# One maximum operation over two PSUM banks per step, three banks for exponentials and dense products, FFN weights in twelve transfers, lag of six steps: an attention and GEGLU block on one core

## The chip, the cores and the metric

The kernel runs on one core of a Trainium2 chip, in one launch. The metric is the device time in microseconds (us), the median of the runs shown. All times come from the kernel's timed runs or from one execution that the hardware profiler took.

## The reference

One transformer block over 2048 tokens of width 512, in bf16, batch 1:

```python
def reference(A_x, A_wqkv, A_wo, B_x, B_w_gate, B_w_up, B_w_down):
    x = A_x
    h = x + A(layernorm(x), A_wqkv, A_wo)
    return h + B(layernorm(h), B_w_gate, B_w_up, B_w_down)

def A(x, wqkv, wo):           # 32 heads of 16
    q, k, v = heads(x @ wqkv)
    p = softmax(q @ k.T * 16 ** -0.5)      # over all 2048 keys
    return (p @ v) @ wo

def B(x, w_gate, w_up, w_down):            # hidden width 1792
    return (gelu(x @ w_gate) * (x @ w_up)) @ w_down
```

## The kernel before

**Units and steps.** The attention is cut into 64 units: 8 groups of 256 queries (`gi`) times 8 slots of four heads (`slot`). A unit has 16 steps ("ticks"). The main loop (L1007 to L1042) runs over ticks and puts out, in each tick, work of two passes:

- **Pass 1**, `p1_pair` and `p1_consume`: two score products of 128 queries by 512 keys, for two heads, and the maximum of each over its 512 keys (L582, VectorE). After a unit's 16th tick, `negm_pre` takes the maximum over the four key blocks (L588), and four small GpSimd operations (L592 to L595) split its negative into three bf16 parts in `ST`. `negm_post` transposes `ST` into `STG` by a DMA (L601) and copies three rows per head from `STG` into spare rows of `QT` by four DMAs (L604). So the scores of pass 2 come out with the maximum already subtracted.
- **Pass 2**, `p2_pair` and `p2_consume`: the transposed scores of the unit again, in two tiles per tick, each of two products of 128 keys by 256 queries (L618); ScalarE takes the exponential of each tile of 128x512 (L628) into `PT`. Every fourth tick `pv_burst` multiplies eight such tiles with V (L644).

Pass 2 of a unit starts `16 + LAGX` ticks after its pass 1, here 26.

**The order on TensorE is written out.** A tick's products of both passes stand between `group_begin` and `group_end`. `group_end` (L108) gathers all semaphore waits of the group and puts them on its first instruction, so none of a tick's score products starts before every bank that the tick writes is free. Only the last product of each pass signals, so ScalarE starts when all four products of pass 2 are through. After the group comes one piece of "dense" work, or a burst of PV products, or, where there is neither, two dummy products (L1001).

**The dense work** is all else on TensorE: the projections of Q, K and V, the transposing back of attention outputs (`item_ofin`), the output projection (`item_oproj`), and for each finished group the FFN (`item_gate`, `item_up`, `item_down`). `Dense.piece()` advances one item by one piece per tick. From four ticks before pass 2 on, `dense.single` is set: an item takes one bank from `banks` when it starts and gives it back when its last piece is put out, and after an item two ticks pass (`PAUSE`). The item's result is taken from the bank by an extra ScalarE operation (`evac_act`), which is put out behind that tick's two exponentials. `item_down` of the first of two tiles takes its bank and then waits for seven ticks.

**The eight PSUM banks.** Banks 0 to 2 are a ring for pass 1, one bank per product (`p1_ring`). Banks 3, 4, 5 and 7 are `Banks.free`, a list out of which pass 2 takes two from the front in each tick, giving them back at its end when the exponentials have been put out, and from which a dense item takes its one. Bank 6 collects the PV products.

```python
while True:                                   # one tick
    P.group_begin("pe")
    t1 = p1_pair(...); t2l = p2_pair(...)     # p2_pair: banks.take() twice
    P.group_end("pe")
    p1_consume(...)                           # L582, and at a unit's end negm_pre, negm_post
    p2_consume(...)                           # L628, banks.give(b) after each
    cost = 0 if pv_tick else dense.piece()    # may take or give a bank
```

**Transfers.** All DMAs are issued by SyncE (SP), in program order; an issue waits for its inputs, and what stands behind it waits too. When the last projection has been put out, `qkv_finished` issues the three FFN weights as three transfers (L482 to L484), since they lie where the projections' operands were.

Of the kernel before, what the change touches and what calls it, by code (L numbers as in the profile page):

```python
# [196 lines left out]
GC = 0.7978845608028654  # L197

NPT = 12
LAGX = 10  # L200
PAUSE = 2


def bass_sequential_preLN__mha_block__geglu_ffn__prompt_kernel(nc, A_x, A_wqkv, A_wo, B_x, B_w_gate, B_w_up, B_w_down, out):
    dbg = None
    with ExitStack() as es:
# [156 lines left out]

        class Banks:
            def __init__(self):
                self.free = [3, 4, 5, 7]
            def take(self):
                return self.free.pop(0)
            def give(self, b):
# [109 lines left out]
        def qkv_finished():  # L479
            fk = [("xnT", t) for t in range(NT)] + ["wqkv"] + [(nm_, dc) for nm_ in ("wq_r", "wk_r") for dc in range(4)] + [("QKS", i_) for i_ in range(4)] + [("QKS2", i_) for i_ in range(2)]  # L480
            dF = rdeps("F", fk)
            P.dma("sp", lambda e: e.dma_start(out=wg_sb[:], in_=B_w_gate.rearrange("(c p) j -> p c j", p=128)), "wg", writes=["wg"], extra_deps=dF)  # L482
            P.dma("sp", lambda e: e.dma_start(out=wu_sb[:], in_=B_w_up.rearrange("(c p) j -> p c j", p=128)), "wu", writes=["wu"], extra_deps=dF)
            P.dma("sp", lambda e: e.dma_start(out=wd_sb[:], in_=B_w_down.rearrange("(c p) j -> p c j", p=128)), "wd", writes=["wd"], extra_deps=dF)  # L484

        qk_n = [0]
        qk_late = []
        def item_projT(b, which, ht, c):
            wr, nm = (wq_r, "wq_r") if which == "q" else (wk_r, "wk_r")
            for dc in range(4):  # L490
                P.op("pe", lambda e, dc=dc: e.matmul(pbank[:, b, :], wr[:, dc, 128 * ht:128 * ht + 128], xnT[:, dc, 512 * c:512 * c + 512], start=(dc == 0), stop=(dc == 3)),  # L491
                     reads=[(nm, dc)] + [("xnT", t) for t in range(4 * c, 4 * c + 4)], writes=[("pb", b)], sig=(dc == 3))
                if dc == 1:
                    yield 2
            si, s2 = qk_n[0] % 4, qk_n[0] % 2; qk_n[0] += 1
            def dst(slot):
                if which == "q":
                    return QT[:, c, slot, :], [("qT", slot, c)] + [("qTaug", slot, c, f_, g_) for f_ in range(2) for g_ in range(4)]
# [24 lines left out]
            qkv_left[0] -= 1  # L523
            if qkv_left[0] == 0:
                qkv_finished()
            return 2
# [38 lines left out]
        def p1_pair(ui, j, gp):  # L565
            gi, slot = units[ui]
            c, hf = gi // 2, gi % 2
            qt, kc = 2 * hf + j // 8, (j // 2) % 4
            tiles = []
            for jj in range(2):  # L570
                g = 2 * gp + jj
                b = p1_ring[0] % 3; p1_ring[0] += 1
                P.op("pe", lambda e, g=g, b=b: e.matmul(pbank[:, b, :], QT[32 * g:32 * g + 32, c, slot, 128 * qt:128 * qt + 128],  # L573
                                                        KT[32 * g:32 * g + 32, slot, 512 * kc:512 * kc + 512], start=True, stop=True, tile_position=(32 * g, 0)),
                     reads=[("qT", slot, c), ("qTaug", slot, c, hf, g), ("kT", slot, kc)], writes=[("pb", b)], sig=(jj == 1))
                tiles.append((b, j // 8, kc, g))
            return tiles

        def p1_consume(ui, tiles):
            par = ui % 2  # L580
            for (b, qt, kc, g) in tiles:
                P.op("dve", lambda e, b=b, qt=qt, kc=kc, g=g: e.tensor_reduce(out=PM[:, par, qt, kc, g:g + 1], in_=pbank[:, b, :], axis=AX.X, op=ALU.max),  # L582
                     reads=[("pb", b)], writes=[("PM", par, qt, kc, g)])

        def negm_pre(ui):
            par = ui % 2
# [10 lines left out]
        def negm_post(ui):  # L597
            gi, slot = units[ui]
            c, hf = gi // 2, gi % 2
            par = ui % 2  # L600
            P.dma("sp", lambda e: e.dma_start_transpose(out=STG[:, par, :].rearrange("p (q s) -> p q s", q=2), in_=ST[:, par].rearrange("p q s -> p (q s)")),  # L601
                  ("stT", par), reads=[("ST", par)], writes=[("STG", par)])
            for g in range(4):
                P.dma("sp", lambda e, g=g: e.dma_start(out=QT[32 * g + 16:32 * g + 19, c, slot, 256 * hf:256 * hf + 256], in_=STG[32 * g + 16:32 * g + 19, par, :]),  # L604
                      ("aug", par), reads=[("STG", par)], writes=[("qTaug", slot, c, hf, g)])

        pv_pending = []
        pt_n = [0]
# [1 line left out]
        def p2_pair(ui, j, gp):  # L610
            gi, slot = units[ui]
            c, hf = gi // 2, gi % 2
            m = j // 2
            tiles = [(banks.take(), m, 2 * gp + jj) for jj in range(2)]
            for i in range(2):
                kt = 2 * m + i
                for (b, _, g) in tiles:
                    P.op("pe", lambda e, g=g, b=b, kt=kt, i=i: e.matmul(pbank[:, b, 256 * i:256 * i + 256], KT[32 * g:32 * g + 32, slot, 128 * kt:128 * kt + 128],  # L618
                                                                        QT[32 * g:32 * g + 32, c, slot, 256 * hf:256 * hf + 256], start=True, stop=True, tile_position=(32 * g, 0)),
                         reads=[("qT", slot, c), ("kT", slot, kt // 4)] + [("qTaug", slot, c, hf, g_) for g_ in range(4)], writes=[("pb", b)],  # L620
                         sig=(i == 1 and g == 2 * gp + 1))
            return tiles

# [69 lines left out]
        def add_ffn(gi):  # L693
# [3 lines left out]
            for k in range(2):  # L697
                dense.add(item_down, gi, k, est=7)

        def load_xres(gi):  # L700
            assert gi < 2 or ffn_done.get(gi - 2), "dense stream too far behind (residual reuse)"
            for k in range(2):
# [15 lines left out]
        def post_hnT(gi, k):  # L718
# [2 lines left out]
                  ("hnT", 2 * gp + k), reads=[("OH", 2 * gp + k)], writes=[("hnT", gp, k)])  # L721
            hn_left[gi] = hn_left.get(gi, 2) - 1
            if hn_left[gi] == 0:
                defer(3, lambda: add_ffn(gi))

        def item_oproj(b, gi, k):
            gp, t = gi % 2, 2 * gi + k
# [71 lines left out]
        def gate_up_mms(b, gi, f, w, nm):  # L799
            hT = hnT_l[gi % 2]  # L800
            hr = [("hnT", gi % 2, k) for k in range(2)]
            for i in range(2):
                fc = 2 * f + i
                for dc in range(4):
                    P.op("pe", lambda e, dc=dc, fc=fc, i=i: e.matmul(pbank[:, b, 256 * i:256 * i + 256], w[:, dc, 128 * fc:128 * fc + 128], hT[:, dc, :], start=(dc == 0), stop=(dc == 3)),  # L805
                         reads=[nm] + hr, writes=[("pb", b)], sig=(dc == 3 and i == 1))
                if i == 0:
                    yield 2

# [37 lines left out]
        def down_mm(b, gi, k, fc):  # L847
            gp = gi % 2
            P.op("pe", lambda e: e.matmul(pbank[:, b, :], GUT[:, fc, 256 * gp + 128 * k:256 * gp + 128 * k + 128], wd_sb[:, fc, :], start=(fc == 0), stop=False),  # L849
                 reads=[("GUT", fc, gp), "wd"], writes=[("pb", b)], sig=False)  # L850
# [156 lines left out]
        while True:  # L1007
# [31 lines left out]
            if pv_tick:  # L1039
                pv_burst(8)  # L1040
            run_deferred(tick)
            tick += 1  # L1042
        run_deferred(tick, flush=True)
        tail_mode[0] = True
# [34 lines left out]
```

## Time and profile before

| | before |
|---|---|
| median of 2 runs | 1392.69 us (1392.41 to 1392.97) |
| profiled execution | 1393.8 us, span 1392.1 us |
| mean granted TensorE clock | 0.991 |
| busy: VectorE / ScalarE / TensorE / GpSimd | 1288.5 / 1235.2 / 1080.1 / 585.9 us |
| first and last product group of pass 1 | 34.4 and 1324.0 us |
| first and last product group of pass 2 | 71.0 and 1353.2 us |
| maxima over pass 1 tiles (L582) | 2048, 1248.9 us |
| exponentials (L628) | 2048, 1103.8 us |

The span is the time from the first to the last instruction of the profiled execution. Busy time is the time in which an engine works on at least one instruction; two instructions of an engine can overlap at their ends, so the mean duration of an instruction times the count is more than the busy time. A row of the timeline gives start, length, engine, line, operation, output and inputs, and in brackets how long the engine sat idle before it and what released it.

### The profile page before, as it was taken

The numbers are of one execution on the slowest core, as the hardware profiler recorded it, in microseconds if no ns is written. First come the engines' busy times: TensorE is split into PE (matmuls) and PEld (weight loads), VectorE is DVE, ScalarE is ACT, GpSimd is POOL, SyncE is SP. The second block draws the span as 40 slices with busy tenths as digits, with TensorE's granted clock in tenths as the row PEclk, the third lists the DMA queues.
The fourth block names the chain that finished last, engine by engine and source line by source line (L and its number), as shares of the span: only waits on it lengthen the run. The fifth ranks groups of instructions, "written<-read, shape, count | busy, mean of one in ns | idle before, by whom it ended". The sixth has DMA issues, their size and how long they took to land.

```text
span 1392.1 us, 33568 instructions
## 1 busy us (share of the span) xinstructions
PE 1080.1 (78%) x12464; PEld 372.1 (27%) x12682; DVE 1288.5 (93%) x2190; ACT 1235.2 (89%) x2409; POOL 585.9 (42%) x830
## 2 busy tenths in 40 slices
PE   4977757777787778777787778777787778877787
PEld 2222212223222222222222322222222322222224
DVE  5999969999999999999999999999999999999912
ACT  4499959999999999999999999899999999999991
POOL 4446611256313562236422662146512563145611
PEclk9999989999999999999999999999999999999999
DMA  3110040100010000000001000100001000100000
GB/s 121 42 29 24 26 164 6 29 5 4 10 21 17 4 6 13 21 11 6 6 13 26 6 6 9 23 13 6 4 13 29 6 3 10 25 14 3 6 15 12
DMA packets 50096, 28.00 MB, mean 20 GB/s; under 512 B 35600, under 2 KB 48400, under 8 KB 49936
## 3 DMA queue, kind: packets, MB, share of 16 engines
q1 hardware_dynamic: 49936, 25.84, 7.0%
q8 instruction: 103, 1.69, 0.5%
q14 instruction: 57, 0.47, 0.1%
HBM read 11.80 MB, written 2.10 MB: 10 GB/s over the span
## 4 chain that ended last, share of the span: by engine, by line
DVE 72%; PE 10%; ACT 8%; issue 7%; DMA 1%; POOL 1%; SPq 1%; POOLq 0%; ACTq 0%; DVEq 0%
DVE PM L582 70%; ACT PT L628 6%; PE pbank L573 3%; PE pbank L618 2%; PE pbank L644 1%; PE pbank L805 1%; DVE NEGM L588 1%; PE pbank L491 1%; PE pbank L849 1%; DVE stats L324 1%; ACT OA L467 1%; DMA OnT<-Otok 1%; PE pbank L730 1%; SPq L604 0%; DMA STG<-ST 0%
## 5 line engine op out<-in xcount | busy, mean ns | idle before, releaser
L582 DVE TENSOR_REDUCE PM<-pbank 128x1 f32<-128x512 f32 x2048 | 1248.9, 685 | 38.1 <-PE pbank L618 26.1
L628 ACT ACTIVATE PT<-pbank 128x512 bf16<-128x512 f32 x2048 | 1103.8, 613 | 87.1 <-PE pbank L618 24.6
L573 PE MATMUL pbank<-KT,QT 32*128 32x512 bf16 x2048 | 399.8, 383 | 208.8 <-DVE PM L582 148.4
L618 PE MATMUL pbank<-QT,KT 32*128 32x256 bf16 x4096 | 401.0, 273 | 2.3 <-ACT PT L628 2.2
L573 PEld LDWEIGHTS pbank<-KT,QT 32*128 32x128 bf16 x2048 | 109.2, 91 | 592.6 <-DVE PM L582 575.0
L1001 PE MATMUL pbank<-ones_bf,ident 128*128 128x512 bf16 x651 | 213.9, 384 | 36.8 <-ACT PT L628 28.9
L644 PE MATMUL pbank<-PT,VA 128*17 128x256 bf16 x4096 | 203.7, 276 | 18.8
L592 POOL CAST ST<-NEGM 128x8 bf16<-128x8 f32 x64 | 13.9, 218 | 318.6 <-DVE NEGM L588 318.6
L670 POOL TENSOR_TENSOR LINV<-OAT,negone 128x16 f32<-128x16 f32 (+1 forms) x32 | 92.0, 2876 | 92.9 <-ACT OAT L467 67.2
L618 PEld LDWEIGHTS pbank<-QT,KT 32*128 32x128 bf16 x4096 | 114.8, 92 | 11.2 <-ACT PT L628 7.0
L644 PEld LDWEIGHTS pbank<-PT,VA 128*17 128x17 bf16 x4096 | 56.5, 87 | 147.0 <-PE pbank L644 92.4
L781 POOL TENSOR_TENSOR w_sb<-g_sb 128x512 f32<-128x512 f32 x49 | 50.9, 1039 | 105.8 <-ACT g_sb L467 105.8
L1001 PEld LDWEIGHTS pbank<-ones_bf,ident 128*128 128x128 bf16 x826 | 49.8, 97 | 100.5 <-ACT PT L628 68.1
L805 PE MATMUL pbank<-hnT_l,wg_sb 128*128 128x256 bf16 x448 | 67.9, 277 | 1.8 <-issue 0.7
L805 PE MATMUL pbank<-hnT_l,wu_sb 128*128 128x256 bf16 x448 | 67.9, 277 | 0.0
L783 POOL TENSOR_TENSOR w_sb<-w_sb,g_sb 128x512 f32<-128x512 f32 x49 | 62.1, 1268 | 4.1
L787 POOL TENSOR_TENSOR th_sb<-th_sb,g_sb 128x512 f32<-128x512 f32 x49 | 62.0, 1264 | 4.1
L843 POOL TENSOR_TENSOR GUT<-th_sb,u_sb 128x512 bf16<-128x512 f32 x49 | 62.0, 1266 | 0.5
L849 PE MATMUL pbank<-wd_sb,GUT 128*128 128x512 bf16 x202 | 56.1, 381 | 5.5 <-PE pbank L618 2.0
L503 POOL TENSOR_SCALAR QT<-QKS,qmask 128x512 bf16<-128x512 bf16 x31 | 48.2, 1562 | 27.3 <-DMA QKS<-QKS 19.5
L786 POOL TENSOR_SCALAR th_sb<-th_sb 128x512 f32<-128x512 f32 x49 | 30.2, 617 | 68.3 <-ACT th_sb L795 68.3
L805 PEld LDWEIGHTS pbank<-hnT_l,wg_sb 128*128 128x128 bf16 x448 | 36.2, 98 | 27.7 <-issue 14.0
(112 smaller groups left out, 639.2 us busy)
## 6 DMA issues: line engine op xcount, KB each, us to landing
QT<-STG SPq DMA_DIRECT2D x256, 1.5 KB
QKS<-QKS SPq DMA_DIRECT2D x32, 112.0 KB, 2.2
x_sb<-in_A_x_dram SPq DMA_DIRECT2D x4, 512.0 KB, 5.6
xres<-in_A_x_dram SPq DMA_DIRECT2D x16, 128.0 KB, 2.2
out_dram<-out_sb SPq DMA_DIRECT2D x16, 128.0 KB, 1.8
wg_sb<-in_B_w_gate_dram SPq DMA_DIRECT2D x1, 1792.0 KB, 7.2
wu_sb<-in_B_w_up_dram SPq DMA_DIRECT2D x1, 1792.0 KB, 12.1
wd_sb<-in_B_w_down_dram SPq DMA_DIRECT2D x1, 1792.0 KB, 16.6
```

What stands on the lines that cost most here:

```text
L573: P.op("pe", lambda e, g=g, b=b: e.matmul(pbank[:, b, :], QT[32 * g:32 * g + 32, c, slot, 128 * qt:128 * qt + 128], KT[32 * g:32 * g + 32, ...
L582: P.op("dve", lambda e, b=b, qt=qt, kc=kc, g=g: e.tensor_reduce(out=PM[:, par, qt, kc, g:g + 1], in_=pbank[:, b, :], axis=AX.X, op=ALU.max ...
L618: P.op("pe", lambda e, g=g, b=b, kt=kt, i=i: e.matmul(pbank[:, b, 256 * i:256 * i + 256], KT[32 * g:32 * g + 32, slot, 128 * kt:128 * kt + ...
L628: P.op("act", lambda e, b=b, pi=pi: e.activation(out=PT[:, pi, :], in_=pbank[:, b, :], func=ACT.Exp), reads=[("pb", b)], writes=[("PT", pi)])
L644: P.op("pe", lambda e, g=g, kt=kt, pi=pi, slot=slot, i=i, col=col: e.matmul(pbank[32 * g:32 * g + 17, PVB, 256 * col:256 * col + 256], VA[ ...
L670: P.op("pool", lambda e: e.tensor_tensor(out=li, in0=oat4[:, :, :, 16], in1=negone[:, 0:8 * ns].rearrange("p (q h) -> p q h", q=2), op=ALU ...
L783: P.op(eng, lambda e: e.tensor_tensor(out=ws, in0=ws, in1=gs, op=ALU.mult), reads=[("w", par), ("g", par)], writes=[("w", par)])
L787: P.op(eng, lambda e: e.tensor_tensor(out=ts_, in0=ts_, in1=gs, op=ALU.mult), reads=[("th", par), ("g", par)], writes=[("th", par)])
L805: P.op("pe", lambda e, dc=dc, fc=fc, i=i: e.matmul(pbank[:, b, 256 * i:256 * i + 256], w[:, dc, 128 * fc:128 * fc + 128], hT[:, dc, :], st ...
L843: P.op("pool", lambda e: e.tensor_tensor(out=o_ap, in0=shp(ts_), in1=shp(us), op=ALU.mult), reads=[("th", par), ("u", par)], writes=o_keys ...
L849: P.op("pe", lambda e: e.matmul(pbank[:, b, :], GUT[:, fc, 256 * gp + 128 * k:256 * gp + 128 * k + 128], wd_sb[:, fc, :], start=(fc == 0), ...
L1001: P.op("pe", lambda e: e.matmul(pbank[:, b, :], ident[:], ones_bf[:, 0:512], start=True, stop=True), reads=["ident", "ones_bf"], writes=[( ...
```

## The change

Five things change together.

- **Pass 1** takes its banks in pairs: 0 and 1, then 2 and 3. One `tensor_reduce` takes the maxima of both banks of a tick (two outputs from 128x2x512) in place of two.
- **Bank 3** goes to pass 1, so the list that pass 2 and the dense items share has three banks, 4, 5 and 7.
- **The subtraction rows**: the four copies from `STG` into `QT` become one GpSimd addition of `STG` (128x256, bf16) onto the unit's half of `QT`.
- **LAGX** is 6 in place of 10.
- **The FFN weights** come in twelve transfers, four each, one at a time in ticks 7, 9, 11 and 13 of every 16; the FFN of a group is put on the list only when all twelve are issued.

```diff
-LAGX = 10
+LAGX = 6
...
-                self.free = [3, 4, 5, 7]
+                self.free = [4, 5, 7]
...
+            wviews = [(wg_sb, ..., "wg", 1), (wu_sb, ..., "wu", 1), (wd_sb, ..., "wd", 4)]
+            for (w, v, nm, step) in wviews:
+                n = w.shape[1]
+                for k in range(0, n, step):
+                    w_pieces.append((w, v, nm, k, min(n, k + step), dF))
+        def w_piece():
+            w, v, nm, k0, k1, dF = w_pieces.pop(0)
+            P.dma("sp", lambda e: e.dma_start(out=w[:, k0:k1, :], in_=v[:, k0:k1, :]), ...)
...
+            b0 = 2 * (p1_ring[0] % 2); p1_ring[0] += 1
             for jj in range(2):
                 g = 2 * gp + jj
-                b = p1_ring[0] % 3; p1_ring[0] += 1
+                b = b0 + jj
...
-            for (b, qt, kc, g) in tiles:
-                P.op("dve", lambda e, ...: e.tensor_reduce(out=PM[:, par, qt, kc, g:g + 1], in_=pbank[:, b, :], axis=AX.X, op=ALU.max), ...)
+            (b, qt, kc, g), (b2, _, _, g2) = tiles
+            P.op("dve", lambda e: e.tensor_reduce(out=PM[:, par, qt, kc, g:g + 2], in_=pbank[:, b:b + 2, :], axis=AX.X, op=ALU.max), ...)
...
-            for g in range(4):
-                P.dma("sp", lambda e, g=g: e.dma_start(out=QT[32 * g + 16:32 * g + 19, c, slot, 256 * hf:256 * hf + 256], in_=STG[32 * g + 16:32 * g + 19, par, :]), ...)
+            q_ap = QT[:, c, slot, 256 * hf:256 * hf + 256]
+            P.op("pool", lambda e: e.tensor_tensor(out=q_ap, in0=q_ap, in1=STG[:, par, :], op=ALU.add), ...)
...
+        def add_ffn_when(gi):
+            if w_pieces or qkv_left[0]:
+                defer(1, lambda: add_ffn_when(gi))
+            else:
+                add_ffn(gi)
...
-                defer(3, lambda: add_ffn(gi))
+                defer(3, lambda: add_ffn_when(gi))
...
             run_deferred(tick)
+            if w_pieces and tick % 16 in (7, 9, 11, 13):
+                w_piece()
```

More of the change, by code (lines that the diff above doesn't have):

```diff
@@ L481, in qkv_finished @@
             dF = rdeps("F", fk)
-            P.dma("sp", lambda e: e.dma_start(out=wg_sb[:], in_=B_w_gate.rearrange("(c p) j -> p c j", p=128)), "wg", writes=["wg"], extra_deps=dF)
-            P.dma("sp", lambda e: e.dma_start(out=wu_sb[:], in_=B_w_up.rearrange("(c p) j -> p c j", p=128)), "wu", writes=["wu"], extra_deps=dF)
-            P.dma("sp", lambda e: e.dma_start(out=wd_sb[:], in_=B_w_down.rearrange("(c p) j -> p c j", p=128)), "wd", writes=["wd"], extra_deps=dF)
+            wviews = [(wg_sb, B_w_gate.rearrange("(c p) j -> p c j", p=128), "wg", 1), (wu_sb, B_w_up.rearrange("(c p) j -> p c j", p=128), "wu", 1),
+                      (wd_sb, B_w_down.rearrange("(c p) j -> p c j", p=128), "wd", 4)]
+            for (w, v, nm, step) in wviews:
+                n = w.shape[1]
+                for k in range(0, n, step):
+                    w_pieces.append((w, v, nm, k, min(n, k + step), dF))
+        w_pieces = []
+        def w_piece():
+            w, v, nm, k0, k1, dF = w_pieces.pop(0)
+            P.dma("sp", lambda e: e.dma_start(out=w[:, k0:k1, :], in_=v[:, k0:k1, :]), (nm, k0), writes=[(nm, k) for k in range(k0, k1)], extra_deps=dF)
         qk_n = [0]
@@ L497, in dst @@
                 if which == "q":
-                    return QT[:, c, slot, :], [("qT", slot, c)] + [("qTaug", slot, c, f_, g_) for f_ in range(2) for g_ in range(4)]
+                    return QT[:, c, slot, :], [("qT", slot, c, f_) for f_ in range(2)]
                 return KT[:, slot, 512 * c:512 * c + 512], [("kT", slot, c)]
@@ L569, in p1_pair @@
             tiles = []
+            b0 = 2 * (p1_ring[0] % 2); p1_ring[0] += 1
             for jj in range(2):
                 g = 2 * gp + jj
-                b = p1_ring[0] % 3; p1_ring[0] += 1
+                b = b0 + jj
                 P.op("pe", lambda e, g=g, b=b: e.matmul(pbank[:, b, :], QT[32 * g:32 * g + 32, c, slot, 128 * qt:128 * qt + 128],
                                                         KT[32 * g:32 * g + 32, slot, 512 * kc:512 * kc + 512], start=True, stop=True, tile_position=(32 * g, 0)),
-                     reads=[("qT", slot, c), ("qTaug", slot, c, hf, g), ("kT", slot, kc)], writes=[("pb", b)], sig=(jj == 1))
+                     reads=[("qT", slot, c, hf), ("kT", slot, kc)], writes=[("pb", b)], sig=(jj == 1))
                 tiles.append((b, j // 8, kc, g))
@@ L580, in p1_consume @@
             par = ui % 2
-            for (b, qt, kc, g) in tiles:
-                P.op("dve", lambda e, b=b, qt=qt, kc=kc, g=g: e.tensor_reduce(out=PM[:, par, qt, kc, g:g + 1], in_=pbank[:, b, :], axis=AX.X, op=ALU.max),
-                     reads=[("pb", b)], writes=[("PM", par, qt, kc, g)])
+            (b, qt, kc, g), (b2, _, _, g2) = tiles
+            assert b2 == b + 1 and g2 == g + 1
+            P.op("dve", lambda e: e.tensor_reduce(out=PM[:, par, qt, kc, g:g + 2], in_=pbank[:, b:b + 2, :], axis=AX.X, op=ALU.max),
+                 reads=[("pb", b), ("pb", b2)], writes=[("PM", par, qt, kc, g), ("PM", par, qt, kc, g2)])
         def negm_pre(ui):
@@ L602, in negm_post @@
                   ("stT", par), reads=[("ST", par)], writes=[("STG", par)])
-            for g in range(4):
-                P.dma("sp", lambda e, g=g: e.dma_start(out=QT[32 * g + 16:32 * g + 19, c, slot, 256 * hf:256 * hf + 256], in_=STG[32 * g + 16:32 * g + 19, par, :]),
-                      ("aug", par), reads=[("STG", par)], writes=[("qTaug", slot, c, hf, g)])
+            q_ap = QT[:, c, slot, 256 * hf:256 * hf + 256]
+            P.op("pool", lambda e: e.tensor_tensor(out=q_ap, in0=q_ap, in1=STG[:, par, :], op=ALU.add), reads=[("STG", par), ("qT", slot, c, hf)], writes=[("qT", slot, c, hf)])
         pv_pending = []
@@ L619, in p2_pair @@
                                                                         QT[32 * g:32 * g + 32, c, slot, 256 * hf:256 * hf + 256], start=True, stop=True, tile_position=(32 * g, 0)),
-                         reads=[("qT", slot, c), ("kT", slot, kt // 4)] + [("qTaug", slot, c, hf, g_) for g_ in range(4)], writes=[("pb", b)],
+                         reads=[("qT", slot, c, hf), ("kT", slot, kt // 4)], writes=[("pb", b)],
                          sig=(i == 1 and g == 2 * gp + 1))
@@ L805, in gate_up_mms @@
                     P.op("pe", lambda e, dc=dc, fc=fc, i=i: e.matmul(pbank[:, b, 256 * i:256 * i + 256], w[:, dc, 128 * fc:128 * fc + 128], hT[:, dc, :], start=(dc == 0), stop=(dc == 3)),
-                         reads=[nm] + hr, writes=[("pb", b)], sig=(dc == 3 and i == 1))
+                         reads=[(nm, dc)] + hr, writes=[("pb", b)], sig=(dc == 3 and i == 1))
                 if i == 0:
@@ L849, in down_mm @@
             P.op("pe", lambda e: e.matmul(pbank[:, b, :], GUT[:, fc, 256 * gp + 128 * k:256 * gp + 128 * k + 128], wd_sb[:, fc, :], start=(fc == 0), stop=False),
-                 reads=[("GUT", fc, gp), "wd"], writes=[("pb", b)], sig=False)
+                 reads=[("GUT", fc, gp), ("wd", fc)], writes=[("pb", b)], sig=False)
         def down_last(b, gi, k):
```

## The prediction

> **What bounds the kernel now.** I read the page first (busy time, the chain that ended last, the groups), then the timeline of single ticks in three places, then the answers on single lines of the kernel.
>
> ```profile
> PE 1080.1 (78%) x12464; PEld 372.1 (27%) x12682; DVE 1288.5 (93%) x2190; ACT 1235.2 (89%) x2409; POOL 585.9 (42%) x830
> ...
> DVE 72%; PE 10%; ACT 8%; issue 7%; DMA 1%; POOL 1%; SPq 1%; POOLq 0%; ACTq 0%; DVEq 0%
> ...
> L582 DVE TENSOR_REDUCE PM<-pbank 128x1 f32<-128x512 f32 x2048 | 1248.9, 685 | 38.1 <-PE pbank L618 26.1
> L628 ACT ACTIVATE PT<-pbank 128x512 bf16<-128x512 f32 x2048 | 1103.8, 613 | 87.1 <-PE pbank L618 24.6
> ```
>
> VectorE sets the end: its maxima are 70% of the chain. But ScalarE is only 53 us less busy, so a faster VectorE soon meets another bound. Which one, single ticks show. Two stretches of FFN work, then of a tick in which ScalarE had to wait:
>
> ```profile
> 1306.71 2.23 ACT L628 ACTIVATE PT<-pbank 128x512 bf16<-128x512 f32 x4
> 1307.36 0.39 PE L573 MATMUL pbank<-KT,QT 32*128 32x512 bf16 x2 [0.26 <-ACT PT L628]
> 1307.69 0.61 PE L805 MATMUL pbank<-hnT_l,wg_sb 128*128 128x256 bf16 x4
> 1308.56 0.39 PE L573 MATMUL pbank<-KT,QT 32*128 32x512 bf16 x2 [0.26 <-DVE PM L582]
> 1308.88 0.86 PE L644 MATMUL pbank<-PT,VA 128*17 128x256 bf16 x16
> 1310.08 0.39 PE L573 MATMUL pbank<-KT,QT 32*128 32x512 bf16 x2 [0.33 <-ACT PT L628]
> 1310.41 0.61 PE L805 MATMUL pbank<-hnT_l,wg_sb 128*128 128x256 bf16 x4
> 1311.31 0.39 PE L573 MATMUL pbank<-KT,QT 32*128 32x512 bf16 x2 [0.28 <-DVE PM L582]
> 1311.54 0.60 ACT L467 ACTIVATE g_sb<-pbank 128x512 f32<-128x512 f32 x1
> ```
> ```profile
> 706.81 2.48 DVE L582 TENSOR_REDUCE PM<-pbank 128x1 f32<-128x512 f32 x4
> ...
> 707.55 0.39 PE L573 MATMUL pbank<-KT,QT 32*128 32x512 bf16 x2 [0.23 <-DVE PM L582]
> ...
> 708.04 1.08 ACT L628 ACTIVATE PT<-pbank 128x512 bf16<-128x512 f32 x2 [0.31 <-PE pbank L618]
> 708.09 1.21 SPq L601 DMA_TRANSPOSE STG<-ST  x1
> ```
>
> In the first, each L573 row opens a tick. An FFN item takes four ticks: a piece (L805), a tick of PV products (L644), the second piece, a pause; its result leaves by a ScalarE operation (g_sb) after the finishing tick's exponentials. The first exponential of the row at 1306.71 lasts 0.60 and ends at 1307.31; the group that waited for it starts 0.05 later. In the second, the group starts at 707.55 and the exponentials 0.49 after; over all ticks where ScalarE sat idle this is 0.48. A pair of exponentials takes 1.08 from start to end, and the second starts 0.49 after the first, so ScalarE alone could do a tick in 0.98. The maxima come every 0.60 (685 mean, overlapping), 1.20 a tick. Today's bank list of four leaves three banks even while a dense item holds one, so a group waits at most for the *first* exponential of the tick before: 0.60 + 0.05 + 0.48 = 1.13, hidden under VectorE's 1.20.
>
> **The change, part by part.**
>
> *One maximum per tick.* Other reads of PSUM by VectorE give the price of an element: copies of 128x512 and 128x272 take 682 and 442 ns, 1.0 ns each; 272 against 136 columns (302 ns) gives 1.03. The second half's 512 elements thus cost 0.53 and the fixed part falls away once: one per 1.13 us. The bounds are 1.11 (1.0 ns) and 1.20 (nothing saved). If VectorE went on setting the pace, 1024 ticks x 0.07 would be a gain of 72 us. With four banks in pairs a group needs only the maximum of two ticks back, so this wait vanishes.
>
> *Three banks for pass 2 and the dense items.* This is what decides. With no item, pass 2 takes two of three in rotation, and a group needs the first exponential of the tick before: 1.13, a "half" tick. While an item holds one, only two are left, the same two each tick. The group waits for the *second* exponential, and since all waits stand on its first instruction, pass 1's products wait as well. Such a "full" tick lasts 1.08 + 0.05 + 0.48 = 1.61, say 1.62, with ScalarE idle for half a microsecond. The tick after the item ended is full too: the bank goes to the list's end and the two before it were both just used. The four-tick item above has three full ticks and one half. The extra ScalarE operation (0.6 long, 0.49 of ScalarE's time) falls into the idle time of the tick after it, so it costs nothing there; the same in front of a half tick makes it 0.98 + 0.49 = 1.47.
>
> How many ticks are full I counted from the trace's products, tick by tick, modulo four. Gate and up: 98 items, 91 with PV between their pieces (3 full ticks each), 7 without (2): 287. `item_ofin`: 31, of which 24 with 3 and 7 with 2: 86. `item_oproj`: 14 x 2 = 28. `item_down`: per group 13 for the first tile (its bank is held through the wait of seven ticks) and 6 for the second, x 7 = 133. Projections: 19 items ran under pass 2; four ticks fewer ahead of it leave some 24, half of each kind: 61. The tail item: 3. Sum 598, say 600 of 1024. The loop of pass 2 is then 600 x 1.62 + 424 x 1.13 = 1451; about 60 extra operations in front of half ticks add 0.34 each, 20: 1471 us. Before, that loop took 1353.2 - 71.0 = 1282.
>
> *LAGX 6.* Pass 2 starts at tick 22 in place of 26; in the trace that tick begins at 66.0 in place of 71.0: 5 us gained, where the ticks of the start, held by two pieces per tick on TensorE (1.29 each), stay as they are. The lag must cover the chain from the unit's last maximum: in the trace the transpose is issued 1.20 after L588 ends and has landed 3.6 after it. Instead of four copies (2.8 of issue, then their landing) comes an addition of 128x256 on GpSimd: L673 of that size takes 0.62, a 128x128 one 0.40 and one of 512 columns 1.27; I take 0.62, so 4.3 after L588. Six half ticks are 6.8, six mixed ones 8.5; there is slack. GpSimd now stands still for the 2.4 us from issue to landing, once per unit, with the gelu operations queued behind; ScalarE's Tanh comes six ticks after the item's end, its three GpSimd operations need 2.9 us, so I cost this at nothing. Cover gone, it is up to 2 us in each of the first six units, where GpSimd still masks Q and K, and in the six whose transposes landed 1 to 1.8 late: 0 to 25 us in all.
>
> *Twelve transfers.* Here one stall goes:
>
> ```profile
> 179.28 10.83 SPq L601 DMA_TRANSPOSE STG<-ST  x1
> ...
> 195.68 2.86 SPq L604 DMA_DIRECT2D QT<-STG  x4
> ...
> 199.65 0.61 PE L573 MATMUL pbank<-KT,QT 32*128 32x512 bf16 x2 [11.32 <-issue]
> ```
>
> The transpose stood behind the three weight transfers and held SP and pass 2: 11.3 idle and four slow ticks after it, some 12 us. Pieces of 0.45 MB in ticks 7 to 13 are through before the next transpose, issued at a tick 0, so all of it goes; the two bounds are 0 and 12. The loop's 1471 has none of it. The wait for the last piece (some 50 ticks after the projections) ends before the first FFN may start, around tick 186.
>
> **The sum.** 66 to the start of pass 2, 1471 loop, and 1392.1 - 1353.2 = 39 for the end as now: 1576 us of span against 1392.1. The profiled execution was 1393.8 and the median 1392.69, the same to 0.1%, so 1576 stands for the time as well. The loss is 600 x (1.62 - 1.20) = 252 in full ticks, against 424 x 0.07 + 12 + 5 and the extra operations that before were not hidden.
>
> **A rule against the change.** Around 0 to 40 us TensorE was busy for 17.69 of 40 us and its granted clock was 0.97; only the 11 us stall took it down, to products of 0.61 for 0.39. A full tick has some 1.0 of 1.62 busy, so I leave the clock full. The Trainium skill, "TensorE: Matmul & The Clock Gate" (section "A second HAM failure mode: psum-queue depth-cycling"), warns that short idle times between groups, while PSUM banks are cycled, can swing the clock between half and full. By that rule each full tick would carry the stall's slow latency. No row here shows it for idle times under a microsecond.
>
> **Rivals.**
>
> 1. *The clock drops in full ticks.* At 199.65 a slow group had its exponentials 0.71 after it, 0.23 more than now: 600 x 0.23 = 138, 1714 us. Against it: the 44% busy stretch at 0.97.
> 2. *The third bank is nearly always free* (the other side: faster). If items gave their bank back before the next group, every tick would be half: 1024 x 1.13 = 1157, plus 267 extra operations x 0.34 = 91: 66 + 1248 + 39 = 1353 us, 2.8% less. A full tick costs 0.49 but hides some extras; the change breaks even at about 105 full ticks. Against it: an item's bank is taken after one tick's group and given back after a later one's, and FFN items alone make 287.
> 3. *ScalarE fills more of the gaps*, with fewer full ticks, as items fall otherwise on the PV ticks (all with 2 full: some 470): 470 x 1.60 + 554 x 1.13 + 35 = 1413; 1518 us.
> 4. *GpSimd's chain is late* at a lag of six: 64 units x 1 us on top, 1640 us. For it: late transposes; against: longer ticks lengthen the lag.
>
> **How the numbers follow.** Forecast 0.74 (own range 1530 to 1630), rival 1 0.05, rival 2 0.05, rival 3 0.08, rival 4 0.06, the rest between them. The range takes in rivals 3 and 4 and leaves out 1 and 2: 1490 to 1650. Two per cent is about what a measurement of this kernel can tell from no change; within it lies only a rival 2 that half holds. Faster 0.04, same 0.02, slower 0.94.
>
> **What would show it.** L582 at 1024 instructions of about 1.2 us, with VectorE no longer the chain's main part; ScalarE idle before L628 released by L618, 200 to 300 us in sum; L573 released by L628 and not L582; FFN stretches at about 1.5 per tick and stretches without dense work at 1.13; no stall near 190 us. I am wrong if FFN stretches stay near 1.25 per tick, or if groups there wait for GpSimd or SP.

## The result, and the profile after

The changed kernel takes 1705.78 us (median of 2 runs, 1705.65 to 1705.91) where the kernel before takes 1392.69 (1392.41 to 1392.97): a ratio of 1.225, 95% interval 1.223 to 1.227. It is slower, as forecast, and by more than forecast: 1576 was the predicted time and 1650 the top of the range. The profiled execution has a span of 1703.9 us and a mean granted clock of 0.923, against 0.991 before.

In the changed kernel the products of pass 1 are L582, those of pass 2 L627, the maximum L592, the exponentials L637, the PV products L653, the dummies L1016, the gate and up products L820. From its page: busy times, the granted clock in 40 slices of the span, the chain that ended last, and three groups:

```profile
PE 1226.6 (72%) x12666; PEld 395.5 (23%) x12666; DVE 1291.9 (76%) x1166; ACT 1277.5 (75%) x2409; POOL 630.9 (37%) x894
...
PEclk9989999997998789998999979987799998999878
...
DVE 55%; PE 31%; ACT 7%; issue 5%; POOL 1%; DMA 1%; SPq 0%; POOLq 0%; DVEq 0%
...
L592 DVE TENSOR_REDUCE PM<-pbank 128x2 f32<-128x1024 f32 x1024 | 1250.3, 1224 | 339.1 <-PE pbank L627 325.5
L637 ACT ACTIVATE PT<-pbank 128x512 bf16<-128x512 f32 x2048 | 1111.7, 595 | 357.9 <-PE pbank L627 282.1
...
L614 POOL TENSOR_TENSOR QT<-QT,STG 128x256 bf16<-128x256 bf16 x64 | 42.7, 667 | 158.4 <-DMA STG<-ST 158.4
```

VectorE has hardly more busy time than before (1291.9 for 1288.5 us) and ScalarE 42 us more, yet they fell from 93% and 89% of the span to 76% and 75%: nearly all of the 312 us are idle time. Half the maxima are gone (1024 in place of 2048), but 1024 of 1224 ns keep VectorE as long as 2048 of 685 did (1250.3 and 1248.9 us), mainly because neighbours no longer overlap. Both engines now stand still for over 300 us, and both wait for the products of pass 2 (L627). So something holds the product groups back. A stretch of the timeline:

```profile
1591.09 0.39 PE L582 MATMUL pbank<-KT,QT 32*128 32x512 bf16 x2 [0.70 <-DVE PM L592]
1591.42 0.86 PE L653 MATMUL pbank<-PT,VA 128*17 128x256 bf16 x16
1591.52 1.23 DVE L592 TENSOR_REDUCE PM<-pbank 128x2 f32<-128x1024 f32 x1 [0.49 <-PE pbank L627]
1591.58 1.08 ACT L637 ACTIVATE PT<-pbank 128x512 bf16<-128x512 f32 x2 [0.63 <-PE pbank L627]
1592.81 0.39 PE L582 MATMUL pbank<-KT,QT 32*128 32x512 bf16 x2 [0.52 <-DVE PM L592]
1593.14 0.61 PE L820 MATMUL pbank<-hnT_l,wu_sb 128*128 128x256 bf16 x4
1593.24 1.23 DVE L592 TENSOR_REDUCE PM<-pbank 128x2 f32<-128x1024 f32 x1 [0.49 <-PE pbank L627]
1593.30 1.08 ACT L637 ACTIVATE PT<-pbank 128x512 bf16<-128x512 f32 x2 [0.63 <-PE pbank L627]
1594.53 0.39 PE L582 MATMUL pbank<-KT,QT 32*128 32x512 bf16 x2 [0.78 <-DVE PM L592]
```

These are two full ticks of 1.72 us, with ScalarE idle for 0.63 ahead of each pair of exponentials. The pair ends at 1591.58 + 1.08 = 1592.66 and the next group's product starts at 1592.81. The forecast had put 0.05 for this release; it is 0.15. Yet the bracket names VectorE. The trace has, in single instructions (start, length, queue, instruction, what it waits for, line):

```
1592.073  0.592  Scalar        ACTIVATE         PT<-pbank              637
1592.703  0.051  Tensor        EVENT_SEMAPHORE  waits for ScalarE
1592.779  0.091  Tensor        LDWEIGHTS        waits for VectorE      582
1592.810  0.371  TensorMatrix  MATMUL                                  582
```

`group_end` gives the group's first weight load several waits. One stays on the load, here VectorE's; ScalarE's stands on a separate semaphore instruction ahead of it. The exponential ends at 1592.665, the separate instruction passes at 1592.703 and lasts 0.051, then the load starts: 0.145 from the end of the exponential to the product. VectorE's wait is for the maximum of two ticks before, since pass 1 uses its two pairs of banks in turn. The Trainium skill says in "Perfetto Trace Analysis" (section "Identifying Dependency Chains") that such instructions may be put in where several engines are waited for; these rows show one.

All ticks of pass 2, by the distance between group starts:

| | ticks | mean us | forecast |
|---|---|---|---|
| full | 476 | 1.716 | 1.62 |
| half | 364 | 1.228 | 1.13 |
| between | 26 | 1.52 | |
| touched by the halved clock | 157 | 1.869 | none |

They add up to 1597 us; the loop runs from 66.2 to 1664.2, 1598 us. The granted clock is at half for 251 us of it, in pieces of 3.4 us and multiples. Two stretches of 40 us from the view by windows (length, busy time and count of PE, PEld, VectorE, ScalarE and GpSimd, then granted clock, DMA share, GB/s):

```profile
340.00:380.00 40.00, 25.71 (x314) 9.75 (x308) 31.03 (x27) 31.78 (x60) 23.23 (x29) 1.00 0.02 5
380.00:420.00 40.00, 27.65 (x276) 8.25 (x270) 27.68 (x24) 28.58 (x54) 16.66 (x20) 0.79 0.01 3
```

In a tick with the clock at half, the exponentials start 0.70 after the group in place of 0.48.

### The profile page after: what moved, and what is told of

It is laid out like the page before. It is cut to its first block, busy times and chain, and to the rows that moved or that the text cites. A ratio compares the mean times of both kernels' runs of the same rounds, so it can differ in the third digit from the quotient of the medians.

```text
span 1703.9 us, 32667 instructions
## 1 busy us (share of the span) xinstructions
PE 1226.6 (72%) x12666; PEld 395.5 (23%) x12666; DVE 1291.9 (76%) x1166; ACT 1277.5 (75%) x2409; POOL 630.9 (37%) x894
## 4 chain that ended last, share of the span: by engine, by line
DVE 55%; PE 31%; ACT 7%; issue 5%; POOL 1%; DMA 1%; SPq 0%; POOLq 0%; DVEq 0%
DVE PM L592 54%; PE pbank L582 13%; PE pbank L627 7%; ACT PT L637 7%; PE pbank L1016 4%; PE pbank L653 2%; PE pbank L864 1%; PE pbank L538 1%; PE pbank L820 1%; PE pbank L499 1%; DVE stats L324 1%; DMA OnT<-Otok 0%; ACT sqj L759 0%; DMA x_sb<-in_A_x_dram 0%; ACT OA L467 0%
## 5 line engine op out<-in xcount | busy, mean ns | idle before, releaser
L592 DVE TENSOR_REDUCE PM<-pbank 128x2 f32<-128x1024 f32 x1024 | 1250.3, 1224 | 339.1 <-PE pbank L627 325.5
L637 ACT ACTIVATE PT<-pbank 128x512 bf16<-128x512 f32 x2048 | 1111.7, 595 | 357.9 <-PE pbank L627 282.1
L582 PE MATMUL pbank<-KT,QT 32*128 32x512 bf16 x2048 | 425.1, 403 | 345.7 <-DVE PM L592 267.1
L627 PE MATMUL pbank<-QT,KT 32*128 32x256 bf16 x4096 | 426.9, 289 | 3.6 <-ACT PT L637 3.4
L1016 PE MATMUL pbank<-ones_bf,ident 128*128 128x512 bf16 x810 | 271.6, 414 | 68.6 <-ACT PT L637 57.0
L582 PEld LDWEIGHTS pbank<-KT,QT 32*128 32x128 bf16 x2048 | 123.7, 91 | 752.6 <-DVE PM L592 507.3
L653 PE MATMUL pbank<-PT,VA 128*17 128x256 bf16 x4096 | 215.2, 289 | 18.8
L627 PEld LDWEIGHTS pbank<-QT,KT 32*128 32x128 bf16 x4096 | 117.0, 94 | 14.8 <-ACT PT L637 7.6
L614 POOL TENSOR_TENSOR QT<-QT,STG 128x256 bf16<-128x256 bf16 x64 | 42.7, 667 | 158.4 <-DMA STG<-ST 158.4
L1016 PEld LDWEIGHTS pbank<-ones_bf,ident 128*128 128x128 bf16 x810 | 51.6, 98 | 185.4 <-PE pbank L627 85.7
L653 PEld LDWEIGHTS pbank<-PT,VA 128*17 128x17 bf16 x4096 | 56.9, 88 | 159.9 <-PE pbank L653 98.3
L820 PE MATMUL pbank<-hnT_l,wg_sb 128*128 128x256 bf16 x448 | 74.8, 297 | 2.4 <-ACT PT L637 0.9
L820 PE MATMUL pbank<-hnT_l,wu_sb 128*128 128x256 bf16 x448 | 72.2, 290 | 0.1
L864 PE MATMUL pbank<-wd_sb,GUT 128*128 128x512 bf16 x224 | 69.4, 424 | 2.8 <-PE pbank L627 0.2
```

What stands on the lines that cost most here:

```text
L592: P.op("dve", lambda e: e.tensor_reduce(out=PM[:, par, qt, kc, g:g + 2], in_=pbank[:, b:b + 2, :], axis=AX.X, op=ALU.max), reads=[("pb", b ...
L637: P.op("act", lambda e, b=b, pi=pi: e.activation(out=PT[:, pi, :], in_=pbank[:, b, :], func=ACT.Exp), reads=[("pb", b)], writes=[("PT", pi)])
L653: P.op("pe", lambda e, g=g, kt=kt, pi=pi, slot=slot, i=i, col=col: e.matmul(pbank[32 * g:32 * g + 17, PVB, 256 * col:256 * col + 256], VA[ ...
L1016: P.op("pe", lambda e: e.matmul(pbank[:, b, :], ident[:], ones_bf[:, 0:512], start=True, stop=True), reads=["ident", "ones_bf"], writes=[( ...
```

## The experiments

The questions were these. Is the loop of ScalarE's exponentials through three banks what sets the tick (theory 1), or the two-bank maximum and its release (theory 2)? Then: what makes a tick 0.1 longer than forecast, what does the clock cost, what do the other parts do by themselves, and would the one maximum have brought its 72 us? Except where a kernel is said to be made from before, its diff is against the changed one. "Before" beside each is the median of the kernel before on the same chip, 1390.6 to 1392.3.

**e1_three_banks: before, with only the bank taken away.** Both maxima per tick, four copies, lag ten and three weight transfers stay.

```diff
-                self.free = [3, 4, 5, 7]
+                self.free = [4, 5, 7]
```

> The kernel before with one edit: pass 2 and the dense items share banks 4, 5, 7 and bank 3 lies idle; pass 1 keeps its ring of three and its two maxima. Theory 1 (the loop from ScalarE's exponential to TensorE's group and back sets each tick once only three banks are shared): half ticks 1.23, full ticks 1.72, some 600 of them full, the clock dropping in places; 1690 to 1740 us, as slow as the changed kernel or slower by the weights' stall. Rival theory 2 (the new two-bank maximum sets the tick, as the waits view of the changed kernel, which names VectorE as the releaser of most groups, would have it): nearly unchanged, 1392 to 1420 us. If half ticks are 1.20 and not 1.23, the half ticks of the changed kernel were VectorE's.

Measured: 1719.14 us, ratio 1.235 (1.231 to 1.239), clock 0.905. Half ticks 1.228 (361), full 1.717 (451), 187 touched by the halved clock. The group of maxima:

```profile
L582 DVE TENSOR_REDUCE PM<-pbank 128x1 f32<-128x512 f32 x2048 | 1297.6, 686 | 295.6 <-PE pbank L618 284.2 <-PE pbank L573 10.6
```

The old maxima at their old duration wait for pass 2 just the same, and both kinds of tick are as long as in the changed kernel to 0.001 us. Theory 1 stands: the lost bank alone costs more than the whole change does, and the two-bank maximum sets neither tick.

**e2_rest: the other parts without the lost bank.** The changed kernel with the four banks, ring of three and two maxima of before; so GpSimd's addition, lag six and twelve transfers are left.

```diff
-                self.free = [4, 5, 7]
+                self.free = [3, 4, 5, 7]
...
-            b0 = 2 * (p1_ring[0] % 2); p1_ring[0] += 1
-                b = b0 + jj
+                b = p1_ring[0] % 3; p1_ring[0] += 1
```

> The changed kernel with the banks and the maxima of before (four shared banks, ring of three, two maxima per tick); the GpSimd addition, the lag of six and the twelve transfers stay. Theory 1: all of the loss is in the banks, so this is faster than before by the stall (12) and the four ticks (5): 1370 to 1380 us, ratio about 0.988. Rival theory 3 (the lag of six or GpSimd's wait for the transpose costs much): over 1400 us, with groups waiting for GpSimd's addition.

Measured: 1397.53, ratio 1.004 (1.003 to 1.006). A gain was expected and a small loss came. From its waits (engine, what stood still, what it waited for: us in all, times, longest):

```profile
POOL QT L612 <- DMA STG<-ST: 169.2, 64, 4.1
...
ACT th_sb L808 <- POOL w_sb L796: 9.8, 9, 2.5
```

The addition itself is never late; it ends at least 0.43 us before its pass 2. But GpSimd stands 2.6 us per unit for the transpose, the gelu operations queue behind, and ScalarE's Tanh waits for them; seven ticks with such a wait last 2.44 us or more, two of these 4.0 and 4.1.

**e8_before_twelve: before, with the twelve transfers alone.** Its diff is `w_piece`, `add_ffn_when` and the pieces' keys, as in the change.

> The kernel before with the FFN weights in twelve transfers and nothing else changed. The stall of 11.3 us at 188 and the slow ticks behind it go: 1378 to 1382 us, ratio 0.990 to 0.994. If the transfers only move the wait: 1388 or more.

Measured: 1378.99, ratio 0.9915 (0.990 to 0.993): 12.7 us less, the stall at 190.

**e9, e15, e16: what the addition and the lag cost.** e9 is e2_rest with the addition put out three ticks later; e15 is e2_rest with lag ten; e16 has both.

```diff
-LAGX = 6
+LAGX = 10
...
-            P.op("pool", lambda e: e.tensor_tensor(out=q_ap, ...))
+            defer(3, lambda: P.op("pool", lambda e: e.tensor_tensor(out=q_ap, ...)))
```

> The run with the banks and maxima of before and the rest of the change (1397 us), with one edit: GpSimd's addition is put out three ticks later, when the transpose has landed. If GpSimd standing still for the transpose, with the gelu operations and then ScalarE's Tanh behind it, ate the gain of the transfers and the lag: 1372 to 1380 us, and GpSimd's wait for the transpose falls from 169 us to under 40. If the lag of six itself was the cost: 1390 or more, with groups released by GpSimd's addition.

> The run with the banks and maxima of before and the rest of the change (1397 us), with the lag back at ten ticks. If GpSimd standing still for the transpose (and Tanh behind it) is what ate the gain: 1393 to 1402 us, the same. If the lag of six did: 1377 to 1385 us.

> The same at a lag of ten, with GpSimd's addition put out three ticks later. At a lag of six that run was late at the start of some units (1396 us); at ten neither the wait nor the lateness should be left: 1376 to 1384 us, as with four copies and twelve transfers (1379). If it stays over 1390, GpSimd's extra work itself costs.

Measured: e9 1396.01, ratio 1.003 (1.002 to 1.005); e15 1409.60, 1.012 (1.010 to 1.013); e16 1378.00, 0.9895 (0.988 to 0.991). Waits of e15, then of e16:

```profile
POOL QT L612 <- DMA STG<-ST: 172.1, 64, 4.1
...
ACT th_sb L808 <- POOL w_sb L796: 16.9, 14, 2.4
```
```profile
POOL QT L612 <- DMA STG<-ST: 61.4, 23, 3.4
```

A longer lag alone does not help (e15): the run is 12 us slower than e2, over both ranges expected; GpSimd stands as long and Tanh waits more. A later addition alone (e9) frees Tanh, though GpSimd's wait for the transpose falls only from 169 to 114 us, where under 40 was expected. But at lag six the addition is now late itself, and units start with ticks of 2.56, in which the first products wait for it:

```profile
PE pbank L581 <- POOL QT L612: 14.0, 9, 1.7
```

With both, Tanh no longer waits for GpSimd and no tick is over 1.6. So at four banks an addition put out at the transpose costs, by the ratios, some 18 us (e2 against e8) to 31 (e15 against e16), through the work queued behind it on GpSimd. The lag of six costs only where the addition is put out later (e9 against e16, 18 us). e16 and e8 do as well as each other; both beat the kernel before by about 1%.

**e4_act_on_group: ScalarE's wait on the weight load, VectorE's on the separate instruction.** Nothing else moves.

```diff
-        e.ops[i0] = (fn, list(need.items()), sig, dsem)
+        e.ops[i0] = (fn, sorted(need.items(), key=lambda kv: kv[0] != "act"), sig, dsem)
```

> The changed kernel with the order of the waits on a tick's group turned: the wait for ScalarE stands on the group's first weight load itself, the wait for VectorE on the separate semaphore instruction ahead of it. Theory 1, with the release term 0.145 us when ScalarE's wait stands on the separate instruction and 0.06 when it stands on the group: half ticks fall from 1.23 to 1.14, full ticks from 1.72 to 1.63; some 1000 ticks x 0.085 = 85 us less, 1610 to 1640 us. Theory 2 (VectorE's maximum sets the tick): unchanged, 1700 to 1710, half ticks 1.23.

Measured: 1621.69, ratio 1.165 (1.160 to 1.170). Half ticks 1.141 (366), full 1.634 (481). From its timeline and its waits:

```profile
1499.78 0.39 PE L582 MATMUL pbank<-KT,QT 32*128 32x512 bf16 x2 [0.44 <-ACT PT L637]
...
1500.21 1.23 DVE L592 TENSOR_REDUCE PM<-pbank 128x2 f32<-128x1024 f32 x1 [0.16 <-PE pbank L627]
1500.27 1.09 ACT L637 ACTIVATE PT<-pbank 128x512 bf16<-128x512 f32 x2 [0.54 <-PE pbank L627]
...
1501.41 0.39 PE L582 MATMUL pbank<-KT,QT 32*128 32x512 bf16 x2 [0.69 <-ACT PT L637]
```
```profile
PEld pbank L582 <- ACT PT L637: 652.7, 997, 1.6
```

84 us go, from the order of two waits. The group now starts 0.05 after the exponentials' end (1500.27 + 1.09 = 1501.36) and 0.03 *before* the maximum ends (1500.21 + 1.23 = 1501.44). So the group does not wait for that maximum, though the same view of the changed kernel had named VectorE:

```profile
PEld pbank L582 <- DVE PM L592: 507.3, 617, 1.2
```

**e14_twelve_act_on_group: the same order of waits in e8.**

> The kernel before with the FFN weights in twelve transfers and ScalarE's wait on the group itself (1379 us with the first alone). Even with four shared banks a dense item leaves three, and some 330 ticks there last 1.23 where VectorE alone would take 1.20: the same release of 0.145 us. If so, they fall to 1.20 and the time by some 10 us: 1364 to 1374. If VectorE's wait, now on the separate instruction, is late in its place: 1379 or more.

Measured: 1398.40, ratio 1.004 (1.003 to 1.006), so 19 us *more* than e8; of the two outcomes expected, the second came. With four banks VectorE's maxima come last, and now they stand on the separate instruction: they come every 0.609 in place of 0.598 (medians), and the median tick went from 1.207 to 1.242. The dearer place hurts whichever engine is last.

**e6_warm and e6b_warm_held: dummies to hold the clock.** e6 adds two dummy products to every tick, into the banks of the next pass 1. e6b does so only while an item holds its bank, sends the usual dummies there too, and adds one.

```diff
+            if p1_ok and p2_started:                                   # e6
+                dummy(2 * (p1_ring[0] % 2), 2)
...
+            h0 = dense.gen is not None                                 # e6b
...
+            held = p1_ok and p2_started and (h0 or dense.gen is not None)
+            nb = 2 * (p1_ring[0] % 2)
-                dummy(banks.free[0], 2 - (cost or 0))
+                dummy(nb if held else banks.free[0], 2 - (cost or 0))
...
+            if held:
+                dummy(nb, 1)
```

> The changed kernel with two more dummy products per tick, in the pass 1 bank pair of the next tick, so that TensorE is busier while a group waits. If the halved clock stretches (157 ticks, mean 1.87) cost some 40 us: granted clock 0.99, 1660 to 1675 us, full ticks all at 1.72. If the clock is not the matter or the dummies are in the way: 1705 or more.

> The changed kernel with TensorE kept busier in full ticks alone: while an item holds its bank, the dummy products go to the next pass 1 pair, which waits for no exponential, and there is one more of them. If the halved clock costs what the slow ticks show (157 ticks, 40 us): granted clock 0.98 or more, full ticks 1.72, 1660 to 1675 us. If the clock cost nothing: 1700 or more at a clock of 0.98.

Measured: e6 1765.33 (1.268, 1.266 to 1.271), clock 0.989; e6b 1650.42 (1.186, 1.184 to 1.188), clock 0.990. In e6 the half ticks rose to 1.30 to 1.43: the added products stood in the way of the next group, so it says nothing of the clock's price. In e6b the half ticks keep 1.228 (401), the full ones are 583 at 1.690, and 21 of the 251 us at half clock are left. The stretch from 380 to 420 us, shown above at 0.79, in e6b:

```profile
380.00:420.00 40.00, 30.74 (x321) 10.60 (x316) 30.47 (x28) 29.56 (x56) 15.07 (x23) 1.00 0.02 4
```

55 us less than the changed kernel, where the clock's 40 were expected. Part of it is not clock: in the down projection's seven waiting ticks the old dummies had waited for an exponential too, and some of those ticks were 2.39 us. And part is the release: the moved dummies have already waited for VectorE, so in 179 of the 583 full ticks the group has ScalarE's wait alone, on the load. One such group starts 0.055 after its exponential (332.744 to 332.799), the one before it, with ScalarE's wait on the separate instruction, 0.143 (331.029 to 331.172). The 179 ticks last 1.63, the other 404 1.72: 179 x 0.09 = 16 us.

**e11_both_terms: e4 and e6b together.**

> The changed kernel with both edits at once: ScalarE's wait on the group itself, and TensorE kept busier in full ticks (alone they gave 1622 and 1650 us). If the release of 0.145 for 0.05 us and the halved clock are all that the forecast of 1576 us had wrong, this run comes to the forecast: 1560 to 1585 us, half ticks 1.14, full ticks 1.61 to 1.63, some 600 of them, clock 0.98 or more. If something else is in the gap, it stays over 1600.

Measured: 1588.30, ratio 1.141 (1.137 to 1.144), clock 0.986; half 1.141 (390), full 1.630 (572). That is 12 us over the forecast; ticks 0.01 longer than forecast make some 10 of them (390 x 0.011 + 572 x 0.010).

**e7_one_tick and e10_three_bank_best: fewer full ticks.** All pieces of an item but the down projection's are put out in one tick, so its bank is held once. e10 is that on e11.

```diff
+            while cost and p2_started and dense.gen is not None and dense.gen.__name__ != "item_down" and dense.pause == 0:
+                if not dense.piece():
+                    break
```

> The changed kernel, but under pass 2 a dense item other than the down projection is put out whole in one tick, so its bank is held over no group and only the tick behind it is full. Theory 1: full ticks fall from some 600 to some 300 (133 for the down projections, one for each of the other 167 items); 300 fewer x 0.49 = 147 less: 1540 to 1580 us, half and full ticks unchanged at 1.23 and 1.72. Theory 2 (the two-bank maximum sets the tick): no change beyond 20 us.

> The changed kernel with three edits: ScalarE's wait on the group, the dummies of the run with a warm clock, and dense items but the down projection put out whole in one tick. Theory 1: fewer full ticks at 1.62 and the rest at 1.14, but the packed items cost new waits for GpSimd, as in the run with that edit alone (1667 us): 1500 to 1560 us, still slower than before.

Measured: e7 1666.75, ratio 1.198 (1.196 to 1.200); e10 1587.22, 1.140 (1.137 to 1.143). The count did what theory 1 says: full ticks at 1.718 fell to 219 and half ones rose to 569. But 156 ticks of 2.4 on average took their place (115 of them touched by the halved clock), some up to 6 us. 14 times ScalarE's copy out of an item's bank waits for GpSimd's gelu operations, 43.8 us in sum; which queue is last in each long tick was not taken apart. On e11 nothing is left of the gain (1500 to 1560 was expected): the granted clock, 0.986 in e11, is 0.959 in e10.

**e12 and e13: would the one maximum have brought 72 us?** Both leave the PV products out, which frees their bank: e12 is before without them, e13 the same with one maximum over two banks *and* four shared banks.

```diff
-                self.free = [3, 4, 5, 7]
+                self.free = [4, 5, 6, 7]
...
+            b0 = 2 * (p1_ring[0] % 2); p1_ring[0] += 1
...
+                P.op("dve", lambda e: e.tensor_reduce(out=PM[:, par, qt, kc, g:g + 2], in_=pbank[:, b:b + 2, :], axis=AX.X, op=ALU.max), ...)
```

> The kernel before without the PV products: two dummy products stand in each burst's place, and the attention output is filled from a constant tile by the same ScalarE operation, so that bank 6 is free. VectorE's maxima still set the pace: 1380 to 1395 us. It is there to be compared with the next.

> The kernel before without the PV products in the same way, with one edit more: one maximum over two banks per tick in banks 0 to 3, while pass 2 and the dense items keep four banks, 4, 5, 6 and 7. Theory 1 (the two-bank maximum is worth what it was costed at, 0.07 us per tick, where its banks are not taken from pass 2): VectorE at 1.13 to 1.14 per tick, ScalarE close behind in FFN stretches (1.17): 1300 to 1330 us. Theory 2 (the two-bank maximum is itself slow, 1.23 per tick): 1400 us or more.

Measured: e12 1390.39 (0.999, 0.998 to 1.000); e13 1370.64 (0.984, 0.982 to 0.987). Nothing hangs on the PV products. The one maximum comes every 1.131 where it isn't held up, as forecast, but the end moves only 20 us, to 1371 in place of 1300 to 1330. Where the maxima set the pace, a tick goes from 1.20 to 1.13. FFN stretches stay at 1.21, as in e12 (1.42, 1.23, 1.18 and 1.02 within an item's four). ScalarE is busy there for 24.0 of 25 us (480 to 505); that its operations are the next limit is likely, not shown. And the output projection's products now wait 14.2 us for the transfer of their input, 0.9 in e12:

```profile
PEld pbank L727 <- DMA OnT<-Otok: 14.2, 7, 3.3
```

## Why the forecast was right in direction and wrong in size

Right:

- *The bank that is lost decides.* e1 has only that edit and is as slow as the whole change. With the two added terms taken out (e11), 1588 stands against 1576.
- *The count.* 600 of 1024 ticks were to be full: 583 in e6b and 572 in e11, where the clock blurs nothing.
- *The maximum.* 1024 instructions of 1224 ns, every 1.131 us where nothing holds them up (e13; forecast 1.13), waiting behind pass 2, not setting the pace.
- *ScalarE's idle time* behind pass 2: 282 us (200 to 300). An FFN item's four ticks last 1.59 on average (1.5): three full, one half.
- *The rim.* Pass 2 starts at 66.2 (66), 39.7 lie behind its last group (39), and there is no stall near 190. The twelve transfers were costed at 12: e8 shows 12.7.

Two signs that the prediction named did not show: VectorE is still 55% of the chain that ended last, and the views name L592, not L637, as the releaser of L582. Both views go by the wait on the load, and e1 and e4 show that it was not the one that ended last.

Wrong:

- **The release of a group by ScalarE, "0.60 + 0.05 + 0.48" and "1.08 + 0.05 + 0.48".** The 0.05 is 0.145. It had been read from the group at 1307.36, where the exponential ended at 1307.31. But a maximum ended at 1307.30, and the separate instruction, with ScalarE's wait, had already passed at 1306.92. So the row shows VectorE's release, whose wait stands on the load itself. ScalarE's stands on the separate instruction. The difference falls on half and full ticks alike: 476 x 0.096 (1.716 - 1.62) + 364 x 0.098 (1.228 - 1.13) = 81 us in the ticks clear of the halved clock. e4, which undoes it, gives 84.
- **"So I leave the clock full."** The granted clock dropped to half for 251 us of the loop. That "only the 11 us stall took it down" was a misreading of the kernel before: there 3.4 us at half, with products of 0.61, also came behind a gap of 1.33 us:

```profile
897.35 0.84 PE L730 MATMUL pbank<-wo_sb,OnT 128*128 128x512 bf16 x2 [1.33 <-DMA OnT<-Otok]
898.12 0.61 PE L573 MATMUL pbank<-KT,QT 32*128 32x512 bf16 x2
```

The Trainium skill's rule weighed there ("TensorE: Matmul & The Clock Gate", section "A second HAM failure mode: psum-queue depth-cycling") held in kind: the clock goes to and fro between full and half. The extent that the prediction drew from it, every full tick, did not come: 157 ticks were touched, not 600. These ticks last some 40 us more than the others would have; e6b, which keeps the clock up, gains 55, of which 16 are the release and some come from dummies that no longer wait.

The two overlap: 84 and then 33 (e4 to e11), or 55 and then 62 (e6b to e11); 117 together of the 130 missed. Of the 22 us that both give, 16 are the 179 ticks of e6b. Rival 1 had 1714, close to what came, but by 0.23 in each full tick from the clock; most of the excess is a release that no rival had, so its nearness is chance.

Of what was costed at nothing, GpSimd's addition was hidden in the changed kernel (it ends at least 2.4 us before its pass 2, and Tanh never waits for it), but under ticks that the lost bank had made long. With four banks that cover is gone and it costs 18 to 31. The "0 to 25" had been given for late additions; in e2 and e15 none is late, and the cost comes through Tanh behind GpSimd, the path that had been put at nothing. And the 72 us of gain was "if VectorE went on setting the pace": e13 shows 20, since the FFN stretches gain nothing, probably for ScalarE's operations there, and the output projection waits for its transfer.

Open: what exactly makes the clock drop. Over 40 us the busy share doesn't tell it (25.71 of 40 us at 1.00, 27.65 at 0.79, the latter with products slowed by the drop itself). Over 3.4 us it tells more. The drops of the changed kernel begin on a grid of 3.41 us. Cut on that grid up to the last group of pass 1, its loop has 30 pieces at full clock with a drop right behind them: TensorE was busy for 51 to 60% of 29 of them, and for 66% of one. Of the 358 pieces with no drop behind them 44 were at 60% or less. In e6b one piece alone is under 64%, at 52%, and behind it comes the only drop of that stretch. So a low share goes before nearly every drop, but does not always bring one; why is not shown. The drops gather in the down projection's waiting ticks, as from 406 to 427 us, and with one product more per tick there, and none that waits for an exponential, they were gone (e6b). Also open: the long ticks of e7 and e10.

## What to carry to other kernels

Before a buffer is given from one loop to another, write down for both which instruction of which earlier step each start then waits for: half a microsecond in 600 steps undid a saving that brought 20 us where it cost no bank (e13). Put the wait that ends last on the instruction itself and the others ahead of it, and read the release term from a row in which only that engine can have been last. Work that waits for a transfer belongs late in an in-order queue, when the transfer has landed, not at its issue, as long as what needs it can wait (e16, against e9).

## What the runs showed of the hardware

- A wait that stands on a separate semaphore instruction ahead of a TensorE group releases it 0.145 us after the awaited exponential ends; a wait on the weight load itself does so in about 0.05. Over 1000 steps that was 84 us, and in a kernel where the other engine is last the same swap cost 19.
- The waits view puts a group's idle time down to the wait on its load, even where a separate semaphore instruction had held it until then: 507 us here bore the wrong engine's name.
- A maximum over two PSUM banks of 128x512 f32 in one instruction takes 1.22 us from start to end and follows its neighbour by 1.131; two single ones come every 0.60. One instruction saves 0.07 per pair.
- The granted clock halved in pieces of 3.4 us in a loop whose idle gaps on TensorE were mostly under a microsecond, and stayed at 0.99 with one product more in each tick in which an item held its bank, and the dummies moved to banks that were free. Of 30 drops, 29 came right behind 3.4 us in which TensorE was busy for 51 to 60%; in the kernel before one came behind a gap of 1.33 us.
